# A fused attention and expert kernel: the order of its first products, head 0's row maxima in two halves, and a lead of coarse units that grows

## The chip, the cores and the metric

The kernel runs on one core of a Trainium2 chip. The metric is the device time of one execution in microseconds, here the median of three runs: 786.41 us (784.92 to 787.25).

## The reference

The reference is a clustered attention, followed by a mixture of experts. A query may only look at keys that have the same nearest centroid.

```python
# B, H, S, D = 4, 8, 768, 64; 16 clusters per head
q_assign = np.argmax(np.einsum('bhsd,hcd->bhsc', q_n, c_n), axis=-1)
k_assign = np.argmax(np.einsum('bhsd,hcd->bhsc', k_n, c_n), axis=-1)
mask = q_assign[:, :, :, None] == k_assign[:, :, None, :]
scores = np.where(mask, scale * np.matmul(q, k.transpose(0, 1, 3, 2)), -1e9)
scores = scores - np.max(scores, axis=-1, keepdims=True)
attn = np.exp(scores)
attn = attn / (np.sum(attn, axis=-1, keepdims=True) + 1e-09)
x = np.matmul(attn, v)            # to [3072, 512]
# then for each token: the best of 4 groups, the best of its 4 experts (16 in all),
# out = weight * (relu(x @ w1[g, e]) @ w2[g, e]), w1: 512 x 1024, w2: 1024 x 512
```

## The kernel before, in words

The 32 pairs of batch and head are numbered 0 to 31 and called heads; two neighbours form a pair, and four share one mask. Fp32 values are split into a high and a low fp16 part, and products are made of high by high, high by low and low by high.

For each pair `load` brings K and Q (`kx`, `qx`, transposed) and `loadv` V. `split(p, w)` makes the high part on ScalarE (L178) and the low part on VectorE (L187) or, for pair 1 at the start, on GpSimd (L184, L185); the parts lie in the tile `parts`. `spread` copies them by DMA to `A` (L210; `QA` and `KA` are its two halves, 64 rows of parts, then the rows of the mask and of the row maximum) and to `B` (L214, L215).

`assign(p)` finds the cluster of each query and key of a pair. 36 products of `parts` with the normalised centroids (L239; `CH` and `CL` are their high and low parts, copied from the centroid transpose L164 at L168 and L169) land in one PSUM bank. Then VectorE runs a chain of six dependent instructions over 128x384 elements: the maximum (`mx`, L244), where it is reached (L246), a descending weight (L247), the maximum of that (`mw`, L249), and the one-hot rows for queries and for keys (L251). `mask_now(h)` transposes the one-hot rows of one head (12 products, L276) and writes them into QA on ScalarE (L278) and into KA on VectorE (L280).

A head's scores are made twice. The *coarse* pass makes 768x768 scores of the high parts in nine units of 512 columns (L302), and VectorE takes each unit's row maxima (L305). `rowmax(h)` joins them (L311), ScalarE negates them (L313), and they go into the last row of QA: for heads 0 and 1 by six transposes and a copy on ScalarE (L318, L319), for the others by a transpose, a copy (L327) and a DMA (L329). The *fine* pass makes the scores in full precision, again nine units a head (`fine(h, u)`, L342 and L343, into `psf`); ScalarE takes the exponential (L347) and GpSimd the low part of it (L349). `av`, five units later, multiplies by V (L368, L369).

The code is written as a loop over the 288 fine units g. With each, coarse units up to a lead ahead of it are issued: `AHEAD0` = 13 units stand ahead of the first fine unit, and the lead grows by one with every four fine units, up to `AHEAD` = 18. Other work (the split and assignment of later pairs, masks, row maxima, the router) is put beside a fine unit by `at(g, f)`. A scheduler then orders the instructions of each engine; it may move an instruction ahead of others where no dependency forbids it, and `tc.issue_after(x)` keeps what is recorded inside it behind x. Each engine then takes its own queue strictly in order, and waits on semaphores. PSUM banks are held in rings of two: `psc` for coarse, `psf` for fine units (heads 0's coarse units use both in turn), `pso`, `psm`.

Ahead of the loop stands the prologue: `warm(8)` multiplies zeros by zeros (`wz`, L102); the centroids are normalised; pair 0 is split, assigned and masked; all nine coarse units of head 0 and four of head 1 run; head 0's row maxima are put in; pair 1 is split, assigned, spread and masked. The first fine unit follows. Attention ends near 430 us; the experts run behind it.

## Time and profile before

| | |
|---|---|
| median of three runs | 786.41 us (784.92 to 787.25) |
| the profiled execution | 782.34 us, of which 780.6 us are the span from its first to its last instruction |
| TensorE (PE) busy | 733.3 us, 94% of the span |
| VectorE (DVE) busy | 612.0 us, 78% |
| ScalarE (ACT) busy | 466.8 us, 60% |
| GpSimd (POOL) busy | 495.6 us, 63% |
| mean granted TensorE clock | 0.978 |
| one DMA into A or B from `parts` | 192.0 KB; of the router weights (`wf`, L538) 40.0 KB |

Busy shares are means over stages that have different limits. A granted clock of 1.00 is 2.4 GHz, 0.50 is 1.2 GHz. In rows of a timeline the first number is the start in us from the span's start, the second the time in us from the start of the first to the end of the last instruction of the row, `xN` the number of instructions, and the bracket the idle time of the engine ahead of the row with what ended it. PEld is TensorE's weight load, which runs beside its products.

### The profile page before, as it was taken

To read this page: it belongs to the slowest core of one execution; us is meant where nothing else is said; L and a number is where in the kernel's file an instruction comes from. 1 tells how busy PE (TensorE), PEld (TensorE's weight loads), DVE (VectorE), ACT (ScalarE), POOL (GpSimd) and SP (SyncE) were. 2 spreads that over 40 slices of the span, in tenths; PEclk is the share of its full clock that TensorE was granted. 3 is DMA by queue.
4 is the path that set the end of the run, shared out by engine and by line. 5 is a ranking of instruction groups with operands and counts; after the bars stand their busy time and mean duration, and the time that the engine had idled before them with its cause. 6 is when DMAs were issued, how large, how long until landed. Compare 5 with 4: busy or idle time off the path is not lost. (4 is left out here: it accounts for less than half of the span.)

```text
span 780.6 us, 26678 instructions
## 1 busy us (share of the span) xinstructions
PE 733.3 (94%) x11086; PEld 626.5 (80%) x11086; DVE 612.0 (78%) x1209; ACT 466.8 (60%) x910; POOL 495.6 (63%) x497
## 2 busy tenths in 40 slices
PE   5899999999999999998999799999999999999991
PEld 3677888878888788886878677887789999999991
DVE  5998879899798988988875465867789888888830
ACT  5567877768777687775895255444344444555530
POOL 9578787778977788776972445434564655565330
PEclk7899999999999999999999999999999999999996
DMA  8856534435344352223312397866688688889600
GB/s 244 204 144 168 148 102 119 137 94 148 104 119 134 94 149 68 55 94 127 92 30 84 85 313 239 272 224 217 209 265 257 218 259 277 285 255 300 194 32 17
DMA packets 80392, 128.28 MB, mean 164 GB/s; under 512 B 8851, under 2 KB 47251, under 8 KB 80264
## 3 DMA queue, kind: packets, MB, share of 16 engines
q1 hardware_dynamic: 74492, 113.12, 48.9%
q0 software_dynamic: 5616, 13.35, 4.9%
q8 instruction: 88, 1.44, 0.8%
q14 instruction: 40, 0.33, 0.1%
q10 hardware_dynamic: 156, 0.03, 0.0%
HBM read 93.20 MB, written 14.11 MB: 137 GB/s over the span
## 5 line engine op out<-in xcount | busy, mean ns | idle before, releaser
L349 POOL TENSOR_TENSOR pl<-p 128x512 f16<-128x512 f32 x278 | 287.3, 1052 | 84.9 <-ACT p L347 80.7
L305 DVE TENSOR_REDUCE mpart<-psc 128x1 f32<-128x512 f32 (+1 forms) x282 | 189.8, 682 | 35.0 <-PE psc L302 32.8
L347 ACT ACTIVATE p<-psf 128x512 f32<-128x512 f32 x288 | 168.7, 595 | 56.1 <-PE psf L343 49.1
L368 PE MATMUL pso<-V,p 128*128 128x65 f16 x1152 | 161.6, 193 | 0.0
L368 PE MATMUL pso<-V,pl 128*128 128x65 f16 x1152 | 161.2, 194 | 0.0
L369 PE MATMUL pso<-V,pl 128*128 128x64 f16 x1152 | 161.0, 191 | 0.0
L369 PE MATMUL pso<-V,p 128*128 128x64 f16 x1152 | 160.8, 191 | 0.0
L342 PE MATMUL psf<-A 82*128 82x384 f16 (+2 forms) x576 | 143.7, 275 | 4.2 <-ACT p L347 2.8
L343 PE MATMUL psf<-B 128*128 128x384 f16 (+2 forms) x576 | 143.7, 274 | 0.0
L369 PEld LDWEIGHTS <-p 128*128 128x128 bf16 x1152 | 112.6, 98 | 21.4 <-issue 0.2
L368 PEld LDWEIGHTS <-p 128*128 128x128 bf16 x1152 | 112.2, 97 | 9.3 <-issue 1.4
L369 PEld LDWEIGHTS <-pl 128*128 128x128 f16 x1152 | 112.8, 98 | 0.7 <-issue 0.4
L302 PE MATMUL psc<-A 80*128 80x512 f16 (+1 forms) x376 | 108.4, 330 | 5.1 <-DVE mpart L305 3.3
L368 PEld LDWEIGHTS <-pl 128*128 128x128 f16 x1152 | 111.2, 97 | 0.3
L953 DVE SCALAR_TENSOR_TENSOR hl<-psh,hh 128x160 f16<-128x160 f32 (+14 forms) x136 | 49.9, 370 | 58.6 <-ACT hh L952 50.4
L952 ACT ACTIVATE hh<-psh 128x160 f16<-128x160 f32 (+14 forms) x136 | 46.6, 347 | 65.7 <-PE psh L950 64.3
L950 PE MATMUL psh<-xT,wh0a 128*128 128x288 f16 (+7 forms) x512 | 74.7, 255 | 0.0
L1011 POOL DMA_INDIRECT out_dram<-y,ri x32 | 38.5, 1203 | 55.1 <-ACT y L1010 48.8
L912 POOL DMA_INDIRECT xg<-xbuf,ri x32 | 43.5, 1359 | 39.8 <-PE psm L922 25.7
L343 PEld LDWEIGHTS <-B 128*128 128x128 f16 x576 | 56.6, 98 | 13.7 <-issue 5.3
L950 PE MATMUL psh<-xT,wh0b 128*128 128x272 f16 (+6 forms) x448 | 65.2, 254 | 0.9 <-ACT xT L924 0.5
L342 PEld LDWEIGHTS <-A 82*128 82x128 f16 x576 | 55.5, 98 | 12.0 <-DMA A<-mr 0.7
(308 smaller groups left out, 1776.9 us busy)
## 6 DMA issues: line engine op xcount, KB each, us to landing
st<-w SPq DMA_DIRECT2D x128, 512.0 KB
B<-parts SPq DMA_DIRECT2D x64, 192.0 KB
kx<-kT SPq DMA_DIRECT2D x16, 384.0 KB
qx<-qT SPq DMA_DIRECT2D x16, 384.0 KB
vx<-vr SPq DMA_DIRECT2D x16, 384.0 KB
A<-parts SPq DMA_DIRECT2D x32, 192.0 KB
xbuf<-xs SPq DMA_DIRECT2D x4, 1536.0 KB
A<-mk SPq DMA_DIRECT2D x56, 24.0 KB
```

The lines of the kernel that those rows point to most:

```text
L302: last["mm"] = nc.tensor.matmul(out=pc[:, off:off + k1 - k0], lhsT=QA[h % 8][0:80, c * P:(c + 1) * P], rhs=KA[h % 8][0:80, k0:k1], start=T ...
L305: nc.vector.tensor_reduce(out=(mp[:, 0, 0:1], mp[:, :, 1], mp[:, 1, 0:1])[i], in_=pc.rearrange("p (a x) -> p a x", a=n), axis=AX.X, op=ALU ...
L342: nc.tensor.matmul(out=o, lhsT=KA[h % 8][0:82, ks], rhs=QA[h % 8][0:82, q0:q1], start=True, stop=False)
L343: nc.tensor.matmul(out=o, lhsT=KBs[h][:, ks], rhs=QBs[h][:, q0:q1], start=False, stop=True)
L347: cfg["exp"] = nc.scalar.activation(out=p32, in_=pf, func=AF.Exp, scale=QK / (SQ * SQ))
L349: lo = (nc.vector if u in (EARLY if h < 2 else DVE_LO[h % 8] if h < NH - 2 else DVE_END) else nc.gpsimd).tensor_tensor(out=pl, in0=p32, in ...
L368: nc.tensor.matmul(out=O[:, col:col + 65], lhsT=p[:, bs], rhs=vh, start=c == 0 and q == 0 and i == 0, stop=False, skip_group_check=True)
L369: nc.tensor.matmul(out=O[:, col:col + 64], lhsT=p[:, bs], rhs=vl, start=False, stop=c == NCH - 1 and i == 1, skip_group_check=True)
L912: self.got = nc.gpsimd.indirect_dma_start(out=xg[0:n].rearrange("p a d -> p (a d)"), out_offset=None, in_offset=bass.IndirectOffsetOnAxis( ...
L950: self.mm = nc.tensor.matmul(out=ph[:, 0:M], lhsT=w[:, k, fs], rhs=xT[:, a, k], start=i == 0, stop=i == 3 * KD - 1)
L952: nc.scalar.activation(out=hh[:, f], in_=ph[:, 0:M], func=AF.Relu)
L953: self.ev = nc.vector.scalar_tensor_tensor(out=hl[:, f], in0=ph[:, 0:M], scalar=0.0, in1=hh[:, f], op0=ALU.max, op1=ALU.subtract)
```

## The change

The prologue is written anew in five places, and the lead follows another rule.

- The centroid copies come ahead of pair 0's split in VectorE's queue. Pair 0's products are recorded with all products of the high parts with CH first, then those with CL, then those of the low parts.
- Pair 0's chain runs once for head 0 and once for head 1, over 192 elements a row each. `mask_now(0)` is recorded between the two.
- Products of zeros are added: six (`warm(6)`) behind pair 0's products, and two ahead of each of head 0's first five coarse units.
- The loop begins when five coarse units are made, not thirteen. With fine unit g, coarse units up to number 2g + 6 are issued, at most 18 ahead of g. Head 0's row maxima go in as two halves, the first (three of six blocks of queries) ahead of the loop, the second in the loop. Pair 1's assignment, spread and masks move to fine units 1 to 5.
- Once there are exponentials, the high part of a split is recorded behind the latest of them. The key mask of odd heads of the first four is written by ScalarE in place of VectorE.

```diff
-    AHEAD, AHEAD0 = 18, 13
+    AHEAD = 18
...
-        nc.vector.tensor_tensor(out=CL[r, :, j], in0=cv[r, :, j], in1=CH[r, :, j], op=ALU.subtract)
+        last["cl"] = nc.vector.tensor_tensor(out=CL[r, :, j], in0=cv[r, :, j], in1=CH[r, :, j], op=ALU.subtract)
...
-        nc.scalar.activation(out=hi, in_=x, func=AF.Copy, scale=SQ)
+        with tc.issue_after(cfg["exp"].ins) if "exp" in cfg else ExitStack():
+            nc.scalar.activation(out=hi, in_=x, func=AF.Copy, scale=SQ)
...
+        if p == 0:
+
+            prods = [(c, t, i) for i in range(3) for t in (1, 0) for c in range(NCH)]
+        else:
+            prods = [(c, t, i) for c in range(NCH) for t in range(2) for i in range(3)]
+        for c, t, i in prods:
+            hi, lo = st[p, t]
+            a, m = ((hi, CH), (hi, CL), (lo, CH))[i]
+            last["sim"] = nc.tensor.matmul(out=sim[:, c, t], lhsT=a[:, c * P:c * P + P], rhs=m[:, pr].rearrange("p h c -> p (h c)"), start=(c, t, i) == prods[0] if p == 0 else i == 0, stop=(c, t, i) == prods[-1] if p == 0 else i == 2, skip_group_check=p == 0)
+        yield
+        if p == 0:
+
+            sim = simt[:, 0:NCH * 4 * C].rearrange("p (g h c) -> p g h c", h=2, c=C)
+            G = 2 * NCH
+            for h in range(2):
+                mx = sm.tile([P, 2 * G], F32, name="mx")[:, 0:G]
+                nc.vector.tensor_reduce(out=mx, in_=sim[:, :, h], axis=AX.X, op=ALU.max)
...
+                yield
+            return
...
+            elif h == 1:
+                nc.scalar.activation(out=dst[64:64 + C], in_=tp[64:64 + C, :S], func=AF.Identity, scale=mscale[64:64 + C], bias=mbias[64:64 + C])
...
+        for _ in range(idle):
+
+            nc.tensor.matmul(out=pc, lhsT=wz[:, 0:P], rhs=wz, start=True, stop=True)
...
-    def rowmax(h):
+    def rowmax(h, c0=0, c1=NCH):
...
-    split(0, 1)
-    split(0, 0)
+    with tc.issue_after(last["cl"].ins):
+        split(0, 1)
+        split(0, 0)
...
-    run(assign(0, ps_f.tile([P, 512], F32, name="psf")))
+    first = assign(0, ps_f.tile([P, 512], F32, name="psf"))
+    next(first)
+    with tc.issue_after(last["sim"].ins):
+        warm(6)
+    next(first)
     mask_now(0, (ps_o, "pso"))
+    run(first)
     spread(0, (0,), part=(1,))
     banks = itertools.cycle(((ps_c, "psc"), (ps_f, "psf")))
-    for u in range(9):
-        coarse(0, u, next(banks))
+    for u in range(5):
+        coarse(0, u, next(banks), 2)
+    run(rowmax(0, 0, NCH // 2))
     mask_now(1, (ps_o, "pso"))
     spread(0, (1,), part=(1,))
-    run(rowmax(0))
...
-    with tc.issue_after(last["mm"].ins), tc.issue_after(last["max"].ins):
-        for u in range(AHEAD0 - 9):
-            coarse(1, u, next(banks))
-        run(assign(1))
-        spread(1)
-        mask_now(2, (ps_m, "psm"))
-        mask_now(3, (ps_m, "psm"))
+    at(1, go, 1, assign(1))
+    at(2, spread, 1)
+    at(4, mask_now, 2, (ps_m, "psm"))
+    at(5, mask_now, 3, (ps_m, "psm"))
...
-    g, n = 0, AHEAD0
+    g, n = 0, 5
...
-            while n < min(9 * NH, g + 1 + min(AHEAD, AHEAD0 + g // 4)):
+            while n < min(9 * NH, g + 1 + AHEAD, 2 * g + 7):
                 coarse(n // 9, n % 9)
-                if n % 9 == 8:
+                if n == 8:
+                    run(rowmax(0, NCH // 2, NCH))
+                elif n % 9 == 8:
                     at(g + 1, go, g + 1, rowmax(n // 9))
                 n += 1
```

The order that the scheduler makes of this, at three places. First TensorE's queue of the change at the low products of pair 0: `parts_240` are the parts of pair 0, `parts_390` those of pair 1, and the rows with L329 are two of the added products of zeros. L239 of before is L244 of the change.

```order
L244 MATMUL psf_249<-CL_195,parts_240 128x32
L329 LDWEIGHTS wz_139
L329 MATMUL psf_338<-wz_139 128x512
...
L244 LDWEIGHTS parts_390 [waits Activation_49]
L244 MATMUL psm_500<-CH_194,parts_390 128x32
L244 LDWEIGHTS parts_390
L244 MATMUL psm_500<-CL_195,parts_390 128x32
L244 LDWEIGHTS parts_240 [waits DVE_49]
L244 MATMUL psf_249<-CH_194,parts_240 128x32
```

Two products of pair 1 now stand between pair 0's products of the high parts and those of the low parts. In the kernel before all 36 products of pair 0 stand together, and those of pair 1 come after the coarse units of head 0.

Next VectorE's queue from the centroids' normalisation to head 0's first coarse maximum, before:

```order
L187 SCALAR_TENSOR_TENSOR parts<-kx,parts 128x768 [waits DMAHW1_49,Activation_49]
L187 SCALAR_TENSOR_TENSOR parts<-qx,parts 128x768 [waits DMAHW2_49,Activation_49]
L168 CAST CH<-psm 64x4x16 [waits PE_49]
...
L244 TENSOR_REDUCE mx<-psf 128x24 [waits PE_49]
L246 TENSOR_TENSOR psf<-psf,mx 128x384 [waits DVE_49]
L247 TENSOR_TENSOR psf<-psf,desc 128x384 [waits DVE_49,Pool_49]
L249 TENSOR_REDUCE mw<-psf 128x24 [waits DVE_49]
L251 TENSOR_TENSOR st<-psf,mw 128x6x2x16 [waits DVE_49,Pool_49]
...
L280 TENSOR_SCALAR A_165<-pso 16x768 [waits PE_49,Pool_49]
L305 TENSOR_REDUCE mpart_198<-psc 128x1 [waits PE_49]
```

and in the change, from behind the low parts, which now follow the copies:

```order
L252 TENSOR_REDUCE mx<-psf 128x12 [waits PE_49]
L254 TENSOR_TENSOR psf<-psf,mx 128x12x16 [waits DVE_49]
L255 TENSOR_TENSOR psf<-psf,desc 128x12x16 [waits DVE_49,Pool_49]
L576 TENSOR_SCALAR WR<-wf 128x80 [waits DMAHW1_49]
L257 TENSOR_REDUCE mw<-psf 128x12 [waits DVE_49]
L577 SCALAR_TENSOR_TENSOR WR<-wf,WR 128x80 [waits DVE_49]
L259 TENSOR_TENSOR st<-psf,mw 128x6x16 [waits DVE_49,Pool_49]
...
L307 TENSOR_SCALAR A_165<-pso 16x768 [waits PE_49,Pool_49]
L257 TENSOR_REDUCE mw<-psf 128x12 [waits DVE_49]
L259 TENSOR_TENSOR st<-psf,mw 128x6x16 [waits DVE_49]
...
L335 TENSOR_REDUCE mpart_198<-psc 128x1 [waits PE_49]
```

The chain's instructions are halved, the router's weights (L576, L577; L540 and L541 before, where they stood behind the first exponentials) have moved in among head 0's half, and the rest of head 1's half stands between head 0's key mask (L307) and its first coarse maximum.

Last ScalarE's queue where it takes up head 2's row maximum, before:

```order
L347 ACTIVATE p32_1098<-psf_1093 128x512 [waits PE_49,Pool_49]
L178 ACTIVATE parts_1494<-kx_1370 128x768 [waits DMAHW3_49,DMAHW4_49,DMAHW2_49,DMAHW5_49,DMAHW1_49,DMAHW0_49]
L313 ACTIVATE mh_976<-m7_974 128x6 [waits DVE_49]
L347 ACTIVATE p32_1129<-psf_1124 128x512 [waits PE_49,Pool_49]
L327 COPY mr_1090<-psm_1059 6x128 [waits PE_49]
```

and in the change:

```order
L378 ACTIVATE p32_1111<-psf_1106 128x512 [waits PE_49,Pool_49]
L378 ACTIVATE p32_1139<-psf_1134 128x512 [waits PE_49,Pool_49]
L343 ACTIVATE mh_986<-m7_984 128x6 [waits DVE_49]
L358 COPY mr_1103<-psm_1072 6x128 [waits PE_49]
```

In both the exponential ahead of the row maximum is the seventeenth, that of fine unit 16. The high part (L178) between the two has gone from here, and the copy that follows no longer has an exponential ahead of it.

## Rows read from the trace of the kernel before

**Rows 1.** Stretches: busy PE, PEld, DVE, ACT, POOL; clock, DMA share, GB/s

```profile
10.00:15.00 5.00, 1.74 (x21) 1.52 (x18) 3.04 (x7) 2.33 (x4) 4.70 (x10) 0.50 1.05 238
...
30.00:40.00 10.00, 8.04 (x167) 6.68 (x165) 9.88 (x19) 5.56 (x9) 4.68 (x4) 1.00 0.92 225
40.00:50.00 10.00, 9.45 (x164) 7.46 (x161) 9.81 (x19) 6.37 (x11) 8.04 (x7) 1.00 0.71 186
50.00:60.00 10.00, 9.86 (x151) 7.32 (x150) 9.39 (x21) 6.50 (x13) 7.50 (x9) 1.00 0.37 104
...
100.00:200.00 100.00, 98.24 (x1899) 81.76 (x1896) 86.80 (x192) 75.11 (x147) 81.07 (x79) 1.00 0.42 117
```

**Rows 2.** The same view in stretches of 1 us, three of them

```profile
22.00:23.00 1.00, 0.71 (x3) 0.47 (x4) 0.94 (x4) 0.23 (x1) 0.32 (x10) 0.50 0.10 22
...
32.00:33.00 1.00, 0.87 (x17) 0.80 (x16) 0.97 (x2) 0.95 (x3) 1.00 (x2) 1.00 0.92 246
...
36.00:37.00 1.00, 1.00 (x27) 0.98 (x26) 1.00 (x3) 0.03 (x1) 0.00 (x0) 1.00 0.91 192
```

**Rows 3.** Timeline of VectorE from 6 to 17 us

```profile
6.38 0.96 DVE L187 SCALAR_TENSOR_TENSOR parts<-kx,parts 128x768 f16<-128x768 f32 x1
...
8.13 0.21 DVE L168 CAST CH<-psm 64x64 f16<-64x64 f32 x1
...
8.86 0.23 DVE L169 TENSOR_TENSOR CL<-psm,CH 64x64 f16<-64x64 f32 x1
10.28 0.56 DVE L244 TENSOR_REDUCE mx<-psf 128x24 f32<-128x384 f32 x1 [1.19 <-PE psf L239]
...
12.80 0.62 DVE L251 TENSOR_TENSOR st<-psf,mw 128x192 f16<-128x192 f32 x2
...
16.08 0.69 DVE L305 TENSOR_REDUCE mpart<-psc 128x1 f32<-128x512 f32 x1 [0.70 <-PE psc L302]
```

**Rows 4.** Timeline of TensorE from 1 to 15 us

```profile
1.24 3.59 PE L102 MATMUL pso<-wz 128*128 128x512 f16 x8 [1.24 <-DVE wz L97]
...
6.66 0.30 PE L164 MATMUL psm<-identf,cn 128*128 128x128 f32 x1 [1.82 <-DVE cn L162]
...
8.88 0.18 PE L239 MATMUL psf<-CH,parts 128*128 128x32 f16 x1 [1.92 <-DVE CH L168]
...
13.21 1.50 PE L276 MATMUL pso<-ident,st 128*82 128x128 f16 x12 [2.97 <-DVE st L251]
```

**Rows 5.** Timeline of ScalarE from 9 to 58 us

```profile
9.97 0.83 ACT L178 ACTIVATE parts<-qx 128x768 f16<-128x768 f32 x1
...
26.54 0.60 ACT L347 ACTIVATE p<-psf 128x512 f32<-128x512 f32 x1 [1.52 <-PE psf L343]
...
52.76 0.20 ACT L313 ACTIVATE mh<-m 128x6 f16<-128x6 f32 x1
...
57.24 1.09 ACT L347 ACTIVATE p<-psf 128x512 f32<-128x512 f32 x2 [1.74 <-PE psf L343]
```

**Rows 6.** Timeline of VectorE from 21 to 52 us

```profile
21.59 0.56 DVE L280 TENSOR_SCALAR A<-pso 16x768 f16<-16x768 f16 x1
...
24.40 0.69 DVE L305 TENSOR_REDUCE mpart<-psf 128x1 f32<-128x512 f32 x1 [0.20 <-PE psf L302]
25.69 0.69 DVE L305 TENSOR_REDUCE mpart<-psf 128x1 f32<-128x512 f32 x1 [0.59 <-PE psf L302]
...
29.47 0.56 DVE L540 TENSOR_SCALAR WR<-wf 128x80 f16<-128x80 f32 x1
29.95 0.34 DVE L251 TENSOR_TENSOR st<-psm,mw 128x192 f16<-128x192 f32 x1
...
51.77 0.16 DVE L311 TENSOR_REDUCE m<-mpart 128x6 f32<-128x18 f32 x1
```

**Rows 7.** Two low parts on VectorE, from the same timeline

```profile
32.30 1.48 DVE L187 SCALAR_TENSOR_TENSOR parts<-kx,parts 128x768 f16<-128x768 f32 x1
...
36.79 0.95 DVE L187 SCALAR_TENSOR_TENSOR parts<-qx,parts 128x768 f16<-128x768 f32 x1
```

More of the change, by code (lines that the diff above doesn't have):

```diff
@@ L219, in splitv @@
         vt = V[p % 4]
-        nc.scalar.activation(out=vt[:, :, :, 64:128], in_=x, func=AF.Copy, scale=SQ)
+        with tc.issue_after(cfg["exp"].ins) if "exp" in cfg else ExitStack():
+            nc.scalar.activation(out=vt[:, :, :, 64:128], in_=x, func=AF.Copy, scale=SQ)
         lo_part(vt[:, :, :, 0:64], x, vt[:, :, :, 64:128], pool)
@@ L233, in assign @@
         sim = simt[:, 0:NCH * 4 * C].rearrange("p (c t x) -> p c t x", c=NCH, t=2)
-        for c in range(NCH):
-            cs = slice(c * P, c * P + P)
-            for t in range(2):
-                hi, lo = st[p, t]
-                for i, (a, m) in enumerate(((hi, CH), (hi, CL), (lo, CH))):
-                    nc.tensor.matmul(out=sim[:, c, t], lhsT=a[:, cs], rhs=m[:, pr].rearrange("p h c -> p (h c)"), start=i == 0, stop=i == 2)
+        if p == 0:
[13 more added lines that the diff above has]
+                nc.vector.tensor_reduce(out=mx, in_=sim[:, :, h], axis=AX.X, op=ALU.max)
+                eq = sim[:, :, h]
+                nc.vector.tensor_tensor(out=eq, in0=eq, in1=mx.broadcast_to([P, G, C]), op=ALU.is_ge)
+                nc.vector.tensor_tensor(out=eq, in0=eq, in1=desc[:, 0:G], op=ALU.mult)
+                mw = sm.tile([P, 2 * G], F16, name="mw")[:, 0:G]
+                nc.vector.tensor_reduce(out=mw, in_=eq, axis=AX.X, op=ALU.max)
+                for t in (1, 0):
+                    last["oh"] = nc.vector.tensor_tensor(
+                        out=ohs[t][:, :, h],
+                        in0=eq.rearrange("p (c t) x -> p c t x", t=2)[:, :, t],
+                        in1=mw.rearrange("p (c t) -> p c t", t=2)[:, :, t].broadcast_to([P, NCH, C]),
+                        op=ALU.is_equal)
+                yield
+            return
         sim = simt[:, 0:NCH * 4 * C].rearrange("p (g c) -> p g c", c=C)
         G = 4 * NCH
-        yield
         mx = sm.tile([P, G], F32, name="mx")
@@ L290, in segs, with coarse @@
         return r
-    def coarse(h, u, pool=(ps_c, "psc")):
+    def coarse(h, u, pool=(ps_c, "psc"), idle=0):
         assert h < 4 or h // 4 in ready
@@ L305, in coarse @@
         nc.vector.tensor_reduce(out=(mp[:, 0, 0:1], mp[:, :, 1], mp[:, 1, 0:1])[i], in_=pc.rearrange("p (a x) -> p a x", a=n), axis=AX.X, op=ALU.max)
-    def rowmax(h):
-        mp = cparts.pop(h)
+    def rowmax(h, c0=0, c1=NCH):
+        mp = cparts[h]
         m7 = sm.tile([P, NCH], F32, name="m7")
-        last["max"] = nc.vector.tensor_reduce(out=m7, in_=mp.rearrange("p j a x -> p (j a) x"), axis=AX.X, op=ALU.max)
+        last["max"] = nc.vector.tensor_reduce(out=m7[:, c0:c1], in_=mp.rearrange("p j a x -> p (j a) x")[:, c0:c1], axis=AX.X, op=ALU.max)
         mh = ozs[0][:, 0, h, :, 64 + C] if h < 2 else sm.tile([P, NCH], F16, name="mh")
-        nc.scalar.activation(out=mh, in_=m7, func=AF.Copy, scale=-1.0 / (SQ * SQ))
+        nc.scalar.activation(out=mh[:, c0:c1], in_=m7[:, c0:c1], func=AF.Copy, scale=-1.0 / (SQ * SQ))
         if h < 2:
             tp = ps_f.tile([P, 512], F32, name="psf").bitcast(F16)
-            for c in range(NCH):
+            cols = slice(c0 * P, c1 * P)
+            for c in range(c0, c1):
                 nc.tensor.transpose(out=tp[0:OZ, c * P:(c + 1) * P], in_=ozs[0][:, 0, h, c], identity=ident)
-            nc.scalar.activation(out=QA[h][64:OZ], in_=tp[64:OZ, :S], func=AF.Identity, scale=oscale[64:OZ], bias=obias[64:OZ])
+            nc.scalar.activation(out=QA[h][64:OZ, cols], in_=tp[64:OZ, cols], func=AF.Identity, scale=oscale[64:OZ], bias=obias[64:OZ])
             ready.add(("max", h))
```

## The prediction, made before the kernel ran

> **What bounds the kernel now.** I read the busy time by stretch first. From 100 us on TensorE is busy for 98.24 of 100 us at a granted clock of 1.00 (2.4 GHz), so what is won or lost before that should show as a shift of everything behind it. The stretches before it look different: from 30 to 60 us VectorE is busy for 9.88, 9.81 and 9.39 of 10 us each, TensorE for 8.04, 9.45 and 9.86 [rows 1]. So the start is paced by VectorE until about 52 us, and by both for some us more. TensorE's clock is at 0.50 (1.2 GHz) between 10 and 15 us [rows 1] and again at 22 us [rows 2].
>
> Then I read the timeline of the first 16 us. VectorE makes the low parts of K and Q of heads 0 and 1 from 6.38 to 8.13 and the centroid copies (CH, CL) from 8.13 to 9.09 [rows 3]. TensorE's centroid product ends at 6.96, but the 36 similarity products start at 8.88, when CH is there [rows 4]. The cluster chain starts at 10.28, ends at 13.42, and the first coarse maximum starts at 16.08 [rows 3].
>
> Last I read VectorE from there to the row maximum of head 2 at 51.77 [rows 6]: the point where both versions have issued 17 fine units (counted in the order of ScalarE, of which the section on the change shows the place), so a fair place to compare. Fine unit 18, the first of head 2, cannot run without it; its exponential comes at 57.24 [rows 5].
>
> **The first products.** With the copies first, VectorE does them right after 6.96: 9.09 − 8.13 = 0.96, so they end near 7.95. The two low parts, 1.75 in all, end near 9.7. The 24 products of the high parts run from about 7.7; 36 products take the 1.4 from 8.88 to the chain's start at 10.28 [rows 3, 4], 0.04 each, so these need 0.96. If the 12 low products followed at 9.7, the chain would start at 9.7 + 0.5 = 10.2, which is no gain on 10.28: the work is the same, only the wait has moved. But the order shows two products of heads 2 and 3 ahead of the low ones, and these wait for ScalarE's high part of `qx`, which ends at 9.97 + 0.83 = 10.80 [rows 5]. TensorE takes its queue in order, so the chain starts at 10.85 + 0.55 = 11.4: **1.1 us later** than before.
>
> **The chain in two halves.** A full chain takes 3.14 (10.28 to 13.42 [rows 3]): four dependent instructions of 384 elements at 0.63 start to start, and two of 192 that take 0.62 together, 0.34 for one alone. 384 elements take 0.56, so 192 more cost 0.22 and an instruction has 0.12 that does not shrink. A half chain is then 4 × 0.41 + 2 × 0.25 = 2.15. Two router-weight instructions now stand inside it; they were 0.56 at 29.47 [rows 6]; between a small instruction of 0.2 and that I take 0.35 each. The half for head 0 ends at 11.4 + 2.15 + 0.7 = 14.2. Its 12 transposes take 1.50 at the low clock [rows 4] and half of it at the high one; the key mask waits for them to 15.0 or 15.7. VectorE fills that with three instructions of head 1's half (1.2), writes the key mask (0.56, as at 21.59 [rows 6]) to about 16.0, and has three more of head 1 (0.9) in its queue ahead of the first coarse maximum: **16.8**, against 16.08, between 16.4 and 17.3.
>
> **VectorE from there to head 2's maximum.** Before: 51.77 − 16.08 = 35.7. Both orders hold the same 29 coarse maxima, 18 chain instructions and six low parts in it. What goes: the two router-weight instructions, 2 × 0.5 (0.56 less the overlap with the next); the key mask of head 1, which ScalarE now writes, 0.6; the idle time of 0.20 and 0.59 at 24.40 and 25.69, where VectorE waits for coarse products that TensorE makes at the low clock [rows 2, 6]. What comes: one more small maximum, 0.16 as at 51.77 [rows 6]. 35.7 − 1.0 − 0.6 − 0.8 + 0.2 = 33.5. New idle time I cannot read; two low parts now wait for ScalarE copies that stand behind exponentials, and the first coarse unit of head 1 waits for two fine units on TensorE. Nothing to 1.0, as the worst of the old waits was 0.59; I take 0.3, since these waits are short. Head 2's maximum comes at 16.8 + 33.5 + 0.3 = 50.6: **1.2 us earlier** than 51.77.
>
> From there ScalarE takes it up at 52.76, 0.83 after it is ready [rows 5, 6], because a high part stands ahead of it; in the new order it follows the exponential directly. I count 0.6 of the 0.83: **1.8 us earlier** at fine unit 18, and as much at the end.
>
> **Edits costed at nothing.** Of the 16 filling products of 3.59 / 8 = 0.45 each [rows 4], four stand ahead of the centroid transpose, and end where it starts (1.24 + 3.59 + 4 × 0.43 = 6.55, against 6.66 [rows 4]): the cover is only 0.1, and past it each us costs one. Two are hidden in the wait for 10.80, six under the chain to 14.2, four under coarse maxima at (21.59 − 16.08) / 9 = 0.61 each [rows 3, 6]. The earlier lead of 18 changes when coarse units are made, not how many; its price is in VectorE's sum, which counts them. The later masks of heads 2 and 3 (fine units 4 and 5 in place of the start) are first wanted by coarse unit 18, which is now issued with fine unit 6, so nothing. High parts behind exponentials: ScalarE is not the bound at any stage, so nothing.
>
> **One rule against it.** A low part takes 0.95 at 36.79, where GpSimd is idle, and 1.48 at 32.30, where GpSimd is busy all along [rows 2, 7]. Exponentials now start near 22.6 in place of 26.54 [rows 5], and GpSimd's subtraction behind each; more of the six low parts will meet it. If three do at the upper price, 3 × 0.53 = 1.6 of the gain is gone. The Trainium skill says on the page "SBUF — State Buffer", section "SBUF: two separate sides", that VectorE and GpSimd hold the shared pair of ports as an exclusive lock, also for a VectorE instruction with two SBUF inputs. By that rule every low part that meets a subtraction is blocked, and the 1.48 agrees.
>
> **The rivals.**
> *TensorE leads.* The first half maximum comes at 16.8 + 6 × 0.61 = 20.5. Before, the exponential came 4.4 after the maximum, which follows the mask at 21.59 + 0.56 (22.15 to 26.54 [rows 5, 6]), at 0.50 clock [rows 2] and behind four coarse units of head 1 that now come later. At full clock and without these about half: 22.6, a lead of 3.9. If it survives, 786.4 − 3.9 = **782.5**. For it: TensorE's 9.86 against VectorE's 9.39 from 50 to 60 us [rows 1]. Against it: VectorE's 9.88 and 9.81 ahead of that.
> *The port*, as above: 1.8 − 1.6 leaves 0.2, **786.2**.
> *The router weights are late.* The first router-weight instruction stands in VectorE's queue inside head 0's half chain, and waits for a load that was asked for at 23 us and now goes behind the two copies of A. VectorE reaches it at 11.4 + 3 × 0.41 = 12.6. The transfers run at 1.05 of the 16 queues' time and some 238 GB/s here [rows 1], so 0.42 MB take 1.8 from the issue near 8.6: in time, if no backlog stands ahead. The row says that there is one, not how long it is. Each us behind 12.6 is a us for everything: the gain is gone at 14.4, and the kernel is 0.3% slower from 16.8; say 17, **789**.
>
> **How the numbers follow.** The profiled execution is 782.34 with a span of 780.6 us, 4.1 below the median of the three runs; I take the difference off both: a span of 778.8, and 786.41 − 1.8 = **784.6**. Chances: the forecast 0.53 (from nothing to 2.7 faster by its bounds: 17.3 or 16.4, idle time 1.0 or 0, 0 or 0.83 on ScalarE), TensorE leads 0.25, the port 0.08, router weights 0.14. The range of 781.5 to 788.2 leaves out the far ends of the second and the last. About 0.3% (2.4 us) can be told from no change. Faster: 0.25 and 0.10 of the forecast, 0.35. Slower: 0.12 of the last and 0.02 for the order of later instructions, which differs up to the end of attention, 0.14. The same: 0.51.
>
> **What will show it.** Right: the chain's first maximum at 11.4, waiting for TensorE, and that for ScalarE's `qx`; the first coarse maximum near 16.8; the first exponential near 22.6 with VectorE still over 9.5 of 10 busy from 30 to 50; head 2's maximum near 50.6. Wrong: a start of the chain at 10.3, or a wait for the router-weight load (the step on the first products, or the third rival); VectorE with idle time from 25 to 50 (then TensorE leads, or a wait that I don't see has come in); a shift at 57 us that is not found at the end.

## The result and the profile after

The changed kernel takes 791.81 us (median of 13 runs), the kernel before beside it 785.9 us (13 runs): a ratio of 1.0084, 95% interval 1.0057 to 1.0111, so by the ratio 6.6 us slower (the two medians are 5.9 us apart). The forecast was 1.8 us faster, its range reached to 788.2. The profiled execution takes 789.45 us, 7.1 more than that of before (782.34).

The busy time by stretch, of the kernel after (the columns of [rows 1]):

```profile
10.00:15.00 5.00, 3.30 (x22) 1.33 (x23) 3.37 (x10) 1.55 (x3) 4.70 (x10) 0.50 1.04 237
30.00:40.00 10.00, 9.36 (x185) 7.90 (x184) 9.43 (x18) 6.16 (x9) 5.95 (x6) 1.00 0.67 155
40.00:50.00 10.00, 7.76 (x76) 5.18 (x76) 8.50 (x17) 3.72 (x7) 2.08 (x2) 0.66 0.67 166
50.00:60.00 10.00, 9.99 (x167) 7.82 (x165) 9.93 (x20) 6.30 (x14) 9.10 (x8) 1.00 0.16 51
100.00:200.00 100.00, 96.85 (x1859) 80.27 (x1856) 85.29 (x189) 73.87 (x145) 79.53 (x78) 1.00 0.43 117
```

Two rows differ from before where nothing was expected. From 40 to 50 us VectorE falls to 8.50, TensorE to 7.76 and its clock to 0.66; and in the steady part, 100 to 200 us, TensorE is busy for 96.85 in place of 98.24.

VectorE's timeline of the start, which answers to [rows 3, 6]:

```profile
11.46 0.36 DVE L252 TENSOR_REDUCE mx<-psf 128x12 f32<-128x192 f32 x1 [1.64 <-PE psf L244]
...
12.60 0.19 DVE L576 TENSOR_SCALAR WR<-wf 128x80 f16<-128x80 f32 x1
...
13.00 1.33 DVE L577 SCALAR_TENSOR_TENSOR WR<-wf,WR 128x80 f16<-128x80 f32 x1
14.26 0.41 DVE L259 TENSOR_TENSOR st<-psf,mw 128x96 f16<-128x96 f32 x2
...
16.39 0.56 DVE L307 TENSOR_SCALAR A<-pso 16x768 f16<-16x768 f16 x1 [0.66 <-PE pso L301]
...
17.71 0.68 DVE L335 TENSOR_REDUCE mpart<-psc 128x1 f32<-128x512 f32 x1
...
21.04 0.69 DVE L335 TENSOR_REDUCE mpart<-psc 128x2 f32<-128x512 f32 x1 [0.59 <-PE psc L332]
22.44 0.69 DVE L335 TENSOR_REDUCE mpart<-psc 128x1 f32<-128x512 f32 x1 [0.71 <-PE psc L332]
23.05 0.15 DVE L341 TENSOR_REDUCE m<-mpart 128x3 f32<-128x9 f32 x1
...
43.96 0.16 DVE L341 TENSOR_REDUCE m<-mpart 128x6 f32<-128x18 f32 x1
...
49.56 1.03 DVE L188 SCALAR_TENSOR_TENSOR V<-vx,V 128x768 f16<-128x768 f32 x1 [0.61 <-ACT V L222]
...
55.42 0.16 DVE L341 TENSOR_REDUCE m<-mpart 128x6 f32<-128x18 f32 x1
```

The chain starts at 11.46 (forecast 11.4). Inside it the second router-weight instruction takes 1.33. The first coarse maximum comes at 17.71 (16.8 was expected, 16.08 before), the first half maximum at 23.05 (20.5). Head 1's maximum comes at 43.96, where it was 39.18 in the kernel before, and head 2's at 55.42 (50.6; before 51.77). Head 1's maximum in the kernel before, and ScalarE's wait for it there:

```profile
39.18 0.16 DVE L311 TENSOR_REDUCE m<-mpart 128x6 f32<-128x18 f32 x1
```

```profile
39.38 0.23 ACT L313 ACTIVATE st<-m 128x6 f16<-128x6 f32 x1 [3.35 <-DVE m L311]
```

What TensorE and GpSimd did in the changed kernel, in their timelines:

```profile
10.87 0.21 PE L244 MATMUL psm<-CH,parts 128*128 128x32 f16 x1 [1.50 <-ACT parts L179]
...
14.81 1.47 PE L301 MATMUL pso<-ident,st 128*82 128x128 f16 x12 [0.83 <-DVE st L259]
...
18.23 1.06 PE L329 MATMUL psf<-wz 128*128 128x512 f16 x2
...
19.52 1.06 PE L329 MATMUL psc<-wz 128*128 128x512 f16 x2
```

```profile
12.65 1.59 POOL L186 TENSOR_TENSOR V<-vx,V 128x768 f16<-128x768 f32 x1
```

The first row is the hoisted product of pair 1, waiting 1.50 us for the high part as forecast. The second row is the 12 transposes for head 0's mask. Two filling products take 1.06, at a clock of 0.50.

ScalarE's timeline, which answers to [rows 5]:

```profile
25.66 0.60 ACT L378 ACTIVATE p<-psf 128x512 f32<-128x512 f32 x1 [0.69 <-PE psf L374]
...
44.15 0.23 ACT L343 ACTIVATE st<-m 128x6 f16<-128x6 f32 x1 [4.26 <-DVE m L341]
...
46.45 0.60 ACT L378 ACTIVATE p<-psf 128x512 f32<-128x512 f32 x1
...
60.00 0.60 ACT L378 ACTIVATE p<-psf 128x512 f32<-128x512 f32 x1
```

These are the first exponential (before 26.54), ScalarE's wait of 4.26 for head 1's maximum, and the exponentials of fine units 8 (before 43.24) and 18 (before 57.24).

If one follows the exponentials of both kernels, unit by unit, the difference has two parts. It is +2.76 at unit 18 and +1.8 from unit 27 to unit 81 (139.82 before, 141.64 after): the start. Then it grows, to +5.71 at unit 234 and +5.36 at the last, unit 287 (418.22 and 423.57): a drift in the steady part. Another 1.8 us come in the experts, where the clock of this execution is lower (0.91 from 440 to 480 us, 0.96 before). The kernels below, whose experts are the same, have anything from −0.3 to +2.8 us there, so I read no cause from it. The drift has a row of its own in the waits of TensorE from 80 to 360 us (us in total, times, longest), the kernel before first, then the changed one:

```profile
PE psc L302 <- DVE mpart L305: 1.1, 3, 0.7
```

```profile
PE psc L332 <- DVE mpart L335: 4.3, 15, 0.5
```

### The profile page after: what moved, and what is told of

It reads as the page before. It is cut to its first block, busy times and chain, and to the rows that moved or that the text cites. A ratio compares the mean times of both kernels' runs of the same rounds, so it can differ in the third digit from the quotient of the medians.

```text
span 787.7 us, 26749 instructions
## 1 busy us (share of the span) xinstructions
PE 741.2 (94%) x11102; PEld 627.9 (80%) x11102; DVE 610.1 (77%) x1215; ACT 467.6 (59%) x913; POOL 493.7 (63%) x497
## 5 line engine op out<-in xcount | busy, mean ns | idle before, releaser
L335 DVE TENSOR_REDUCE mpart<-psc 128x1 f32<-128x512 f32 (+1 forms) x286 | 193.1, 683 | 34.6 <-PE psc L332 31.5
L378 ACT ACTIVATE p<-psf 128x512 f32<-128x512 f32 x288 | 170.5, 596 | 60.2 <-PE psf L374 47.7
L399 PE MATMUL pso<-V,pl 128*128 128x65 f16 x1152 | 163.3, 194 | 1.0 <-POOL pl L380 0.9
L400 PE MATMUL pso<-V,pl 128*128 128x64 f16 x1152 | 163.1, 191 | 0.0
L948 POOL DMA_INDIRECT xg<-xbuf,ri x32 | 41.5, 1298 | 42.5 <-PE psm L958 28.2
L986 PE MATMUL psh<-xT,wl0a 128*128 128x288 f16 (+7 forms) x256 | 64.0, 255 | 0.0
```

The source lines that it names most:

```text
L335: nc.vector.tensor_reduce(out=(mp[:, 0, 0:1], mp[:, :, 1], mp[:, 1, 0:1])[i], in_=pc.rearrange("p (a x) -> p a x", a=n), axis=AX.X, op=ALU ...
L378: cfg["exp"] = nc.scalar.activation(out=p32, in_=pf, func=AF.Exp, scale=QK / (SQ * SQ))
L399: nc.tensor.matmul(out=O[:, col:col + 65], lhsT=p[:, bs], rhs=vh, start=c == 0 and q == 0 and i == 0, stop=False, skip_group_check=True)
L400: nc.tensor.matmul(out=O[:, col:col + 64], lhsT=p[:, bs], rhs=vl, start=False, stop=c == NCH - 1 and i == 1, skip_group_check=True)
L948: self.got = nc.gpsimd.indirect_dma_start(out=xg[0:n].rearrange("p a d -> p (a d)"), out_offset=None, in_offset=bass.IndirectOffsetOnAxis( ...
L986: self.mm = nc.tensor.matmul(out=ph[:, 0:M], lhsT=w[:, k, fs], rhs=xT[:, a, k], start=i == 0, stop=i == 3 * KD - 1)
```

## Experiments

Each time is a ratio to runs of the kernel before on the same chip. The other columns are of one profiled execution: the start of the first coarse maximum and of head 1's maximum, the exponential's shift against the kernel before at fine units 8, 27, 81 and 287, and TensorE's waits for row maxima from 80 to 360 us. One profiled execution need not be a typical one: y1's was the slowest of its 12 (786.66 us, their median is 782.19), z4's the fastest (784.03, median 786.42). So the other columns show what happened in one execution, and the ratio shows what an edit is worth.

| kernel | ratio [95%] | coarse | head 1 | unit 8 | 27 | 81 | 287 | waits |
|---|---|---|---|---|---|---|---|---|
| before | 1 | 16.08 | 39.18 | 0 | 0 | 0 | 0 | 1.1 |
| after | 1.0084 [1.0057, 1.0111] | 17.71 | 43.96 | +3.21 | +1.88 | +1.81 | +5.36 | 4.3 |
| x1 | 1.0093 [1.0062, 1.0124] | 17.71 | 44.52 | +3.69 | +6.76 | +6.49 | +6.06 | 0.4 |
| x2 | 1.0066 [1.0034, 1.0098] | 15.80 | 39.32 | +0.61 | +1.39 | +1.33 | +4.54 | 3.9 |
| x3 | 1.0022 [0.9998, 1.0047] | 18.18 | 42.71 | +1.88 | +1.08 | +1.03 | +2.99 | 3.4 |
| x4 | 1.0001 [0.9981, 1.0020] | 15.47 | 40.87 | +0.01 | −1.38 | −1.45 | +0.75 | 4.2 |
| y1 | 0.9974 [0.9954, 0.9993] | 15.58 | 42.16 | +1.39 | +0.92 | +0.71 | +1.72 | 1.1 |
| y2 | 1.0044 [1.0023, 1.0066] | 17.10 | 42.84 | +2.09 | +0.75 | +0.68 | +2.83 | 3.5 |
| y3 | 1.0025 [1.0006, 1.0044] | 16.74 | 42.85 | +2.10 | +0.77 | +0.72 | +2.89 | 3.2 |
| z4 | 1.0036 [1.0016, 1.0057] | 17.71 | 40.01 | −1.18 | +0.25 | −0.45 | +1.91 | 3.6 |
| y6 | 1.0003 [0.9977, 1.0030] | 15.25 | 40.84 | +0.01 | +3.44 | +3.12 | +2.71 | 0.4 |
| z7 | 0.9966 [0.9950, 0.9982] | 15.02 | 36.76 | −4.43 | +0.50 | −0.02 | −0.41 | 1.1 |
| z5 | 0.9970 [0.9946, 0.9994] | 15.15 | 36.98 | −4.20 | −1.81 | −1.27 | −1.83 | 1.1 |
| w1 | 0.9974 [0.9959, 0.9989] | 15.59 | 39.07 | −2.12 | −1.12 | +0.72 | +0.45 | 1.1 |

**x1 and x2: the high parts behind exponentials.** x1 is the changed kernel without that rule, x2 the kernel before with it alone.

```diff
-        with tc.issue_after(cfg["exp"].ins) if "exp" in cfg else ExitStack():
-            nc.scalar.activation(out=hi, in_=x, func=AF.Copy, scale=SQ)
+        nc.scalar.activation(out=hi, in_=x, func=AF.Copy, scale=SQ)
```

(And the same for V; x2 adds what x1 takes away.)

> The changed kernel, but the high part of a split is no longer kept behind the latest exponential. My theory: the shift against the kernel before grows from 1.8 us at fine unit 81 to 5.7 at unit 234 because of this rule, by way of low parts that come later and crowd VectorE when it should take coarse maxima. Then the shift stays near 1.8 to 2.2 at unit 234, TensorE's waits for coarse maxima from 80 to 360 us fall from 4.3 us to near 1, and the time is some 3.7 us below that of the changed kernel. Rival: the drift is the prologue's or the lead's doing (coarse units lie differently to the masks for good); then the shift at unit 234 stays above 5 and the time stays.

> The kernel before, with only that rule for the high parts added. My theory: no difference worth more than 1 us at fine unit 27, then a drift to some 3.7 us at unit 234, and a time 3.7 us above that of the kernel before. Rival (prologue or lead): within 1 us of the kernel before throughout.

The waits of TensorE from 80 to 360 us, of x1 and then of x2:

```profile
PE psc L330 <- DVE mpart L333: 0.4, 2, 0.2
```

```profile
PE psc L304 <- DVE mpart L307: 3.9, 12, 0.5
```

The drift belongs to the rule: x2 has it without any other edit (+1.33 at unit 81, +4.54 at the last), x1 lacks it. But x1's time did not fall, and at unit 234 its shift is +6.33, which is the sign that the rival was given; what it stands for is another cost. By unit 27 x1 stood 4.9 us behind the changed kernel, 1.8 of that by unit 18, ahead of which two high parts of 0.84 now stand. ScalarE's timeline of x1, and SyncE's queue (the issue of the load of `qx`):

```profile
67.89 0.84 ACT L178 ACTIVATE parts<-qx 128x768 f16<-128x768 f32 x1 [2.16 <-issue]
```

```profile
62.44 0.43 SPq L80 DMA_DIRECT2D qx<-qT  x1
```

Freed from the rule, a high part moves ahead of exponentials and ScalarE stands for 2.16 us ahead of it. The load of a `qx` was issued 5.45 us before the high part starts; in the kernel before the corresponding load left at 57.37. In front of it on SyncE's queue are the eight mask copies, from 55.74 on, in the kernel before from 51.68 on. That the wait is for this load fits, but the profile doesn't name it. So the rule costs 3 to 4 us in the steady part, and at the start it seems to cover a late load. In x2 it costs something at the start too: +1.39 at unit 27, where at most 1 was expected.

**x3: no filling products beside coarse units.**

```diff
-        coarse(0, u, next(banks), 2)
+        coarse(0, u, next(banks))
```

> The changed kernel without the two products of zeros ahead of each of the first five coarse units. My theory: at the low clock those ahead of units 3 and 4 hold TensorE for 0.86 us each, and VectorE's idle time of 0.17, 0.59 and 0.71 us from 19.7 to 23 is theirs. Without them the first half maximum comes at about 21.7 in place of 23.05, head 1's maximum about 1.3 us earlier than 43.96, and the time is 0.5 to 1.5 us lower. Rival: the products raise the clock and so pay for themselves; then the clock rises later than 22 us and the first exponential is not earlier than 25.66.

The first half maximum came at 22.11 (forecast 21.7; VectorE's timeline), against 23.05, although the first coarse maximum was 0.5 later:

```profile
22.11 0.15 DVE L341 TENSOR_REDUCE m<-mpart 128x3 f32<-128x9 f32 x1
```

From first coarse to first half maximum it is 3.9 us, not 5.3: the products that were to cost nothing cost 1.4 here. Nor did they raise the clock in these two executions: it is 0.50 from 15 to 20 us with and without them, and 0.80 and 0.79 from 20 to 25. The first exponential came earlier, at 24.38, so the rival is out. By the last unit x3 stands 2.4 us ahead of the changed kernel. The ratio fell by 0.0062 or 4.9 us, more than the 0.5 to 1.5 expected; by the intervals of the two ratios this difference is good to about 2.9 us, so what goes beyond 2.4 is not clear of noise.

**x4, y2, y3: pair 1's products and the router weights.** x4 holds pair 1's products behind pair 0's, and the two router-weight instructions behind head 0's first maxima. y2 is the first edit alone, y3 the second.

```diff
-            last["sim"] = nc.tensor.matmul(out=sim[:, c, t], ...
+            with tc.issue_after(last["sim"].ins) if p == 1 else ExitStack():
+                last["sim"] = nc.tensor.matmul(out=sim[:, c, t], ...
...
+    cfg["max0"] = last["max"]
     R.setup()
...
+        with self.tc.issue_after(self.cfg["max0"].ins):
+            nc.vector.tensor_scalar(out=self.WR[:, 0], in0=wf, ...
+            nc.vector.scalar_tensor_tensor(out=self.WR[:, 1], in0=wf, ...
```

> The changed kernel with the products of heads 2 and 3 kept behind those of heads 0 and 1 and the two router-weight instructions kept behind the first half maximum. My theory: the chain starts at 10.3 in place of 11.46, and the 1.33 us that the second router-weight instruction takes inside the chain goes; the first coarse maximum starts at 15.5 in place of 17.71. Of these 2.2 us some 1 to 2 are left at fine unit 27 and at the end. Rival: VectorE's sum behind this point sets the pace only together with head 1's maxima, and what is won here is lost in waits before 44 us; then head 1's maximum stays within 0.5 of 43.96.

> Pair 1's products held behind pair 0's, nothing else of x4. Theory (each step of the first 18 us costs what it takes): the cluster chain starts near 10.3 in place of 11.46, the router-weight instructions still stand inside it, the first coarse maximum comes near 16.6 in place of 17.71, and the end is 1.1 us earlier than the changed kernel: ratio to the kernel before 1.007. Rival (x4's gain of some 6 us hangs on TensorE's clock, which only x4 had back at 1.00 by 15 us, and which needs both edits): the chain moves but the clock stays at 0.50 past 20 us, and the time stays within 0.6 us of the changed kernel.

> The two router-weight instructions held behind head 0's first half of maxima, nothing else of x4. Theory (each step costs what it takes): the chain still starts at 11.4, head 0's one-hot ends near 13.2 in place of 14.67, the first coarse maximum comes near 16.3 in place of 17.71, and the end is 1.5 us earlier: ratio 1.0065. Rival (as for the run with pair 1's products alone): the clock stays low past 20 us and the time within 0.6 us of the changed kernel.

VectorE's timelines of x4, y2 and y3, in this order:

```profile
10.38 0.36 DVE L253 TENSOR_REDUCE mx<-psf 128x12 f32<-128x192 f32 x1 [0.41 <-PE psf L245]
...
15.47 0.68 DVE L336 TENSOR_REDUCE mpart<-psc 128x1 f32<-128x512 f32 x1
```

```profile
12.18 0.47 DVE L577 TENSOR_SCALAR WR<-wf 128x80 f16<-128x80 f32 x1 [0.68 <-DMA wf<-wr]
...
12.82 1.52 DVE L578 SCALAR_TENSOR_TENSOR WR<-wf,WR 128x80 f16<-128x80 f32 x1
14.27 0.41 DVE L260 TENSOR_TENSOR st<-psf,mw 128x96 f16<-128x96 f32 x2
```

```profile
13.23 0.42 DVE L259 TENSOR_TENSOR st<-psf,mw 128x96 f16<-128x96 f32 x2
...
22.14 0.23 DVE L579 SCALAR_TENSOR_TENSOR WR<-wf,WR 128x80 f16<-128x80 f32 x1
```

In x4 the chain and the first coarse maximum came where they were expected, and head 1's maximum at 40.87, so the rival is out. x4 gains 3.3 us on the changed kernel by unit 81, more than the 1 to 2 expected, and is as fast as the kernel before. In y2 the chain starts 1.2 us earlier, and head 0's one-hot rows are no earlier at all (14.27, against 14.26): VectorE now waits 0.68 for the load of the router weights, which is the third rival's mechanism, and then 1.52 in the second instruction. What y2 gains came later (its first coarse maximum at 17.10; 16.6 was forecast), with TensorE's clock at 0.66 from 15 to 20 us and 1.00 from 20 to 25 where the changed kernel has 0.50 until near 22. In y3 head 0's one-hot rows start at 13.23 and the first coarse maximum comes 1.0 earlier. Both are 1.1 us earlier than the changed kernel at unit 81, within 0.4 of the forecasts, and 2.5 us earlier at the last unit. The ratios fell by 0.0040 and 0.0059 (3.1 and 4.6 us), which agrees with that within their intervals. The rivals' low clock past 20 us did not come (1.00 from 20 to 25 us in both), and by the ratios the edits pay no more together (0.0083) than apart (0.0099 in all), so x4's gain does not hang on having both.

**z4: the work of pairs 2 and 3 four fine units later**, in the changed kernel.

```diff
+        if Q == 1:
+            pos = [x + 4 for x in pos]
...
-    at(0, split, 2, 0)
-    at(1, split, 2, 1)
+    at(4, split, 2, 0)
+    at(5, split, 2, 1)
```

> The changed kernel with the planned jobs of the second pair of pairs (splits, cluster chains, copies, mask) four fine units later each. Theory (head 1's maximum at 43.96 is the gate, and it is late because VectorE has pair 2's cluster chain of 2.5 us and two more low parts of 0.87 ahead of it, which before came behind): head 1's maximum comes some 4 us earlier, near 39.8, fine unit 8's exponential near 42.5, head 2's maximum near 51 in place of 55.42, and the end 3 to 4 us earlier, ratio 1.004. Rival (the work is only put off): the shift at fine unit 8 falls but comes back when head 4's mask is wanted, by fine unit 36, and the time stays at 1.008. Other rival (head 1's maximum is late because the start and the low clock are): it still comes after 43.

VectorE's timeline:

```profile
40.01 0.16 DVE L341 TENSOR_REDUCE m<-mpart 128x6 f32<-128x18 f32 x1
...
50.42 0.15 DVE L341 TENSOR_REDUCE m<-mpart 128x6 f32<-128x18 f32 x1
```

Head 1's maximum comes 3.95 earlier (forecast 39.8), fine unit 8 4.4 earlier, head 2's maximum 5.0, and 2.3 of it are left at unit 81: the rival of work put off takes about half there. At the last unit 3.5 us are left, and the ratio, 1.0036, is the 1.004 of the theory. The first coarse maximum and the clock up to 20 us (0.50) are those of the changed kernel, so a late start alone is not the cause: head 1's maximum moves with what VectorE has to do ahead of it. z4 takes away more than the change had put there, though. From the first coarse maximum to head 1's it is 23.1 us in the kernel before, 26.3 in the changed one and 22.3 in z4.

**y1, y6: the rule only for the first 27 fine units**, in x4; y1 also without the filling products beside coarse units.

```diff
-        with tc.issue_after(cfg["exp"].ins) if "exp" in cfg else ExitStack():
+        with tc.issue_after(cfg["exp"].ins) if "exp" in cfg and now[0] < 27 else ExitStack():
```

> The edit of x4, without the filling products beside coarse units, and with the copies behind exponentials only while fewer than 27 fine units are issued. Theory (the costs add): x4 stood 0.75 us behind the kernel before at the end of attention, of which 2.4 came after fine unit 81 (the drift of the rule) and the filling products are worth about 1. Without both the end comes 2 to 3 us ahead of the kernel before, so about 781 against its 783.6, and TensorE's waits for row maxima between 80 and 360 us fall from 4.2 us to under 1.5. Rival (the rule of the later units also keeps copies from standing ahead of exponentials while their transfers are late, as the 2.16 us wait at 67.89 in x1 showed): the shift rises by 2 to 4 us between fine units 17 and 27, and the time is 784 to 786.

> The edit of x4 with the copies behind exponentials only while fewer than 27 fine units are issued, and with the filling products kept: against y1 the filling products alone differ. Theory (the filling products cost only while TensorE's clock is low; with the early start of x4 they keep it at 1.00 through the first 27 us, where y1's fell to 0.50 between 21 and 27): the clock stays at 1.00 from 15 to 40 us, fine unit 8 comes at 43.3 as in x4 and not at 44.62 as in y1, and the end is some 1 us ahead of y1: ratio 0.996. Rival (filling products cost wherever they stand, as x3 against the changed kernel showed): the end is 1 us behind y1, ratio 0.9985.

The drift is gone in both (waits 1.1 and 0.4; the shift from unit 81 to unit 234 goes from +0.71 to +0.53 and from +3.12 to +2.99). By the ratio y1 is faster than the kernel before, near what was expected (0.9974; 781 us for 783.6 is 0.9967). In its profile, of the slowest run, 2 us are lost behind unit 270 (a shift of −0.24 there, +1.72 at the last), for which I have no cause. y6 is not faster: from unit 18 to unit 27 its shift rises from +1.40 to +3.44, as the rival said for y1, and its ratio of 1.0003 lies above both forecasts. ScalarE's timeline shows in it what x1 showed, where y1 has 0.47:

```profile
64.53 0.84 ACT L179 ACTIVATE parts<-qx 128x768 f16<-128x768 f32 x1 [1.98 <-issue]
```

The copies recorded behind unit 27 are free to move ahead to there, so the rule's cover seems to be wanted for them too. On the filling products the pair decides nothing: y6 had the clock of 1.00 from 15 to 40 us that was expected and fine unit 8 at 43.25, but w1 below shows that a start's clock can differ by as much without any edit.

**z7, z5, w1: all of it together.** z7 is y6 with z4's edit, z5 the same without filling products, w1 is z5 with the row of head 3's maxima sent from ScalarE's queue.

```diff
-        (nc.scalar if h == 2 else nc.sync).dma_start(...
+        (nc.scalar if h in (2, 3) else nc.sync).dma_start(...
```

> y6 and the planned jobs of pairs 2 and 3 four fine units later. Theory (head 1's and head 2's maxima are the gates of the start whatever comes before them): 2 to 3 us more than y6, as z4 gained on the changed kernel: ratio 0.993. Rival (with an early start TensorE is the limit from 40 us on, so that an earlier maximum gains nothing): the same as y6, 0.996.

> z7 without the filling products. Theory (as for y6): 1 us behind z7, with the clock at 0.50 for some us between 20 and 30 us: ratio 0.9945. Rival (filling products cost wherever they stand): 1 us ahead of z7.

> z5 with one edit more: the copy of head 3's maxima, which stood behind the eight mask copies of the second pair of pairs on SyncE's queue (56.73 to 61.74, so it was issued at 62.25 though the row was ready at 60.6), is issued by ScalarE, as head 2's is. Theory (the 3.16 us that ScalarE waited at fine unit 27 in z5, where the lead over the kernel before fell from 5.2 to 1.8 us, come from that place in the queue): unit 27 starts 1.5 us or more earlier, near 64.3 in place of 65.93, and the lead at fine unit 81 grows from 1.3 to 2.8: ratio 0.995. Rival (the unit waits for the masks or for TensorE all the same, or ScalarE loses what it takes to issue the copy): no gain, 0.997 as z5.

z7 and z5 can't be told apart, so neither theory on the filling products is borne out. Both are 0.3% faster than the kernel before, less than the 0.55 to 0.7% expected. Against y6, z7 gains 0.0037 or 2.9 us, the 2 to 3 that z4's edit was expected to bring. z7 and z5 are 3 us and more ahead of everything above at fine unit 8, but lose most of it by fine unit 27. ScalarE's timeline there, z5 and then w1 (the first row of each is the copy of head 3's maxima):

```profile
60.32 0.24 ACT L359 COPY mr<-psm 6x128 f16<-6x128 f16 x1
...
65.93 1.26 ACT L379 ACTIVATE p<-psf 128x512 f32<-128x512 f32 x2 [3.16 <-PE psf L375]
```

```profile
62.50 0.24 ACT L359 COPY mr<-psm 6x128 f16<-6x128 f16 x1
...
66.61 1.26 ACT L379 ACTIVATE p<-psf 128x512 f32<-128x512 f32 x2 [1.19 <-PE psf L375]
```

ScalarE's wait fell from 3.16 to 1.19, but part of that is only w1's later start, which brings ScalarE to the wait later. What the place behind the masks costs is better read from the copy on: the row's transfer was issued 1.93 us behind the copy's start in z5 (62.25) and 0.27 in w1 (62.77), and unit 27 follows the copy by 5.61 and 4.11 us. That is the 1.5 us expected. But unit 27 came no earlier (64.3 was expected) and the ratio did not fall, because w1's start was 2 us later: the windows of z5 and then of w1 from 10 to 15 and 25 to 30 us show a clock of 1.00 and 1.00 in the one, 0.50 and 0.64 in the other, though the two programs order the same instructions up to that copy, past 55 us.

```profile
10.00:15.00 5.00, 4.28 (x25) 2.44 (x23) 3.96 (x13) 1.92 (x3) 4.70 (x10) 1.00 1.04 238
25.00:30.00 5.00, 4.96 (x60) 3.62 (x59) 5.00 (x11) 4.81 (x9) 3.98 (x5) 1.00 0.81 269
```

```profile
10.00:15.00 5.00, 4.28 (x27) 2.49 (x27) 3.57 (x11) 2.27 (x4) 4.70 (x10) 0.50 1.04 222
25.00:30.00 5.00, 5.00 (x39) 3.32 (x37) 3.83 (x7) 2.82 (x5) 3.09 (x4) 0.64 0.96 299
```

## Why the prediction was wrong

At fine unit 18 the forecast was −1.8 us and the profile shows +2.76. Of these 4.5 us, 0.9 came before the first coarse maximum and 4.0 from idle time of VectorE behind it; the work of VectorE and ScalarE's part came out 0.1 and 0.3 better. The rest came behind unit 18. Of the signs that the prediction named for being wrong, two were there: VectorE idle between 25 and 50 us, by a wait that was not seen, and a shift near 57 us that is not the one at the end.

- **The first products: right.** 11.46 for 11.4, with the two waits that were named. x4 and y2 undo it: 10.4 and 10.3.
- **The chain in two halves: the term "0.35 each" for the router weights was mis-sized.** Without them the half for head 0 takes 2.13 in y3, for 2.15 forecast; with them it took 3.21 (11.46 to 14.67) for 2.85. The second instruction took 1.33 (0.58 in the kernel before). It ends at 14.33, just behind GpSimd's low part of V (12.65 + 1.59 = 14.24). In x3 and y2 it began earlier, took 1.53 and 1.52, and ended at 14.33 and 14.34 as well; with GpSimd in small constants it took 0.23 (y3). The rows of the kernel before held such a wait too: the 0.56 at 29.47, from which the term was sized, ended at 30.03, and the 0.58 at 31.07, where GpSimd's subtractions ended at 29.98 and 30.97. So they were no price of the instruction alone. The Trainium skill says on the page "SBUF — State Buffer", section "SBUF: two separate sides", that of a VectorE instruction with two SBUF inputs and a GpSimd instruction that reads SBUF, whichever starts first holds the shared port pair for its whole instruction and the other blocks; these rows agree. The port was looked for only at the low parts, where it did not matter: the six took 6.8 us, 6.7 before. Of the miss of 0.9 (17.71 for 16.8, beyond the bound of 17.3) some 0.4 are this. The rest is mainly the 12 transposes: they ran at the low clock (1.47), and the forecast had put the key mask's end between its two cases, at 16.0; it came at 16.95.
- **VectorE's sum to head 2's maximum: the work was right, the idle time of 0.3 was the step that failed.** From 17.71 to 55.42 VectorE was busy for 33.41 us (forecast 33.5) and idle for 4.3. About half (2.1) is waiting for coarse products from 18 to 27 us, 1.5 of it by 22.44, at the low clock and behind filling products. Another 1.5 lie between 44 and 50 us. There head 1's maximum is the gate. Its negation stands on ScalarE's queue ahead of the exponential of fine unit 8, although that unit is still head 0's: fine units 0 to 7 have run by 34.3 us, and ScalarE waits 4.26 us for a maximum that VectorE makes behind four low parts of pairs 2 and 3 and pair 2's whole chain. While that lasts TensorE runs dry: from 39 to 42 us it is busy for 0.54, 0.26 and 0.02 of each us, and from 43 to 49 us its clock is 0.50 (1.00 in the kernel before from 40 to 50). The gate was there before the change too, with a wait of 3.35 us; it stood behind fine unit 5. By the new lead the last coarse unit of head 1 is recorded with fine unit 6 in place of 4, so its maximum moves from beside unit 5 to beside unit 7: units 6 and 7 come 8 us earlier, and unit 8 comes 3.21 later. The lead was priced by how many units it makes; what it put ahead of the gate was not.
- **Why head 1's maximum is 4.78 us later.** 1.63 came with the first coarse maximum. From there VectorE was busy for 23.41 us in place of 22.04, which is the work put ahead of the gate (21 coarse maxima for 20, four low parts for three, the whole of pair 2's chain for its first two instructions, less the router weights and a mask), and idle for 2.84 in place of 1.06. z4 shows that less work ahead of it brings the maximum forward; how far each of the three parts would have cost time alone is not shown.
- **From head 2's maximum to unit 18: right.** The change saves 0.89 there: 4.58 us (55.42 to 60.00) for 5.47. The 0.6 was low.
- **"As much at the end": wrong.** The high parts behind exponentials were costed at nothing, on the ground that ScalarE is not the bound. It is not, but behind a high part stand VectorE's low part, then the coarse maximum, then TensorE. Rows show the ends of that line: VectorE waits for ScalarE's high parts (2.5 us in 5 waits from 80 to 360 us, none before), and TensorE 4.3 in place of 1.1 for row maxima. x2 gives 3.2 us of drift to this edit alone; taking it away past unit 27 removes it (y1 and y6, up to unit 234). The links between, wait by wait, are argued.
- **The fillers: "four under coarse maxima" was wrong too.** x3 prices them at 1.4 us to the first half maximum. Two of them with one coarse unit take 1.3 us at the clock of 0.50 (18.23 to 19.52), more than the 0.61 of a maximum that was to hide them.
- **The rivals.** TensorE leads: no; the first exponential was at 25.66, not 22.6. Nor does such a lead survive: in x4 the first exponential came at 21.74, 4.8 us ahead of the kernel before, and fine unit 8 at 43.25 for 43.24, behind head 1's maximum. The port at low parts: no. The late router weights: not in the changed kernel, but 0.68 us in y2. The result, slower, had 0.14 for other reasons.

What stays open: whether the ratios of x3 and y3, which fell by some 2 us more than the shift at their last unit, hold a gain that the profiles don't show, since this lies within the intervals; and whether filling products are worth anything once the start is early.

## What to carry to other kernels

A sum of busy times along the engine that seems to bound a stretch can be right to 0.1 us and still miss: when the order is changed, look for the one result that the next stage waits for, and count what now stands ahead of it on its engine's queue. An edit on an engine that is not the bound is free only if nothing on the way from its output to the engine that is the bound gets later. A wait that is removed in one place shows the next: here the load of the router weights behind the hoisted products, and, once head 1's maximum came earlier, the mask copies ahead of head 3's row. And before a row serves as the price of an instruction, look at what ran beside it: the rows that priced the router weights held waits for GpSimd.

## What the runs showed of the hardware

- VectorE's 128x80 instruction with two inputs took 0.23 us beside GpSimd's small constants (y3), and 1.06 to 1.53 beside its low part of V, where it ended 0.09 to 0.10 us behind that in every kernel (14.33 for 14.24 in the changed one). The instruction ahead of it, which has one input, showed the same: 0.19 in the changed kernel, where it began 0.05 us ahead of that low part (12.60 and 12.65), and 1.57 in w1, where it began 0.08 behind another (19.42 and 19.34) and ended at 20.99 for 20.93.
- Two programs with the same instructions up to 55 us (z5, w1) had a granted clock of 1.00 and of 0.50 between 10 and 15 us, and their fine unit 8 came at 39.03 and 41.12. A start of one profiled execution is not known to better than 2 us here.
